# Cluster-masked attention and a maxout layer on one core: the fourth pair of the first batch gets its cluster mask another way, and VectorE shares copies in a new order

## The chip, the core and the metric

The kernel runs on one core of a Trainium2 chip. The metric is the device time of one execution, in microseconds (us). Three runs of the kernel before took 711.57, 712.71 and 713.95; the median is 712.71. Besides, one execution was recorded by the hardware profiler.

The engines are called as in the profile: PE is the matrix engine (TensorE) and PEld its loading of weights, DVE is VectorE, ACT is ScalarE, POOL is GpSimd, SP is SyncE, which only issues DMA transfers here. Each engine works through its own list of instructions in order and waits on semaphores where it needs what another one makes.

## The reference

Four batches, eight heads, 768 tokens of 64 elements. Every query and every key is assigned to the nearest of 16 centroids of its head, and a query sees only the keys of its own cluster:

```
q_assign = argmax(einsum('bhsd,hcd->bhsc', q / |q|, c / |c|), -1)
k_assign = argmax(einsum('bhsd,hcd->bhsc', k / |k|, c / |c|), -1)
scores = where(q_assign[..., :, None] == k_assign[..., None, :], q @ k.T / 8, -1e9)
x = softmax(scores) @ v            # as rows of tokens: 3072 x 512
h = maximum(maximum(x @ w1, x @ w2), x @ w3)      # 3072 x 768
out = h @ w_out                                   # 3072 x 512
```

All is float32. The kernel multiplies in float16 and splits numbers into an upper half (the float16 cast) and a lower half (what the cast left over), with a power of two as scale for each tensor, so that products of halves add up to about float32.

## The kernel before

**Tiling.** A *pair* is two heads of one batch; a batch has four. The 768 queries are six tiles of 128; a batch has two blocks of three tiles. A *visit* is one pair and one block: 32 visits, first the four pairs of block one of a batch, then those of block two, with six *steps* each (two heads by three tiles), 192 in all.

**A step** (`tile_units`, L1145). PE makes the scores of 128 queries against 768 keys in a two-bank PSUM tile `big`, of which there are three (L1160, L1162; the second adds the lower halves and the mask). DVE takes the row's maximum and writes the shifted scores back (L1171), ACT takes the exponential (L1177) and the row sum, ACT casts the upper half `hl` (L1180), and DVE or POOL subtract it for the lower half (L1183). SP then turns both halves with a transposing DMA (L1186), and the attention product (L1111) reads them. For the even steps below 40 (`BY_PE`), PE turns the float32 rows instead (L1208), and ACT (L1214) and DVE (L1216) take the halves out of PSUM into `pt`. In later batches the rows are also divided by their sum (POOL or ACT L1227, or within L1233 and L1236).

**A pair's preparation** (`prep`, L624, and `mask_rows`, L485). q and k are loaded as two tiles `stage` with the elements of q and k in the partitions and the tokens along the row. DVE or ACT takes the maximum of the absolute values, a short chain of one-column instructions (`pow2_units`, L374 to L400, with one tiny matmul) makes a power of two out of it, the halves are written to `qk` (L710 to L727). For the mask, the pair's centroids are multiplied with the `stage` tiles: in batch 0 by four float32 matmuls with the centroids `cwf` as weights (L700), which give the scores with clusters in the partitions in a `big` tile. On DVE follow: a 32 by 32 block transpose (L497), so that the 16 scores of a token lie along a row, the maximum (L506), the subtraction of it (L509), the rank of the first that equals it (L515, L518), the one-hot row (L522), its scaling to 0 or a large negative number in two copies (L535) and a block transpose back (L546). Four row copies put the result under the q and k rows of `qk`, where the score product adds it: by DVE for the very first pair (`fast`, L567), by DMA for all others (L569). `cl_t` and `cl_m` are the tiles of this chain.

**Weights and the feed-forward part.** `weights` (L956) brings the three hidden matrices in 18 pieces: loads, an upper-half cast (`top`, L928 or L930), a conversion to float32 on DVE (`wf`, L934), scaling, halves (L891, L893, L950). After the four visits of a block follows `ffn` (L1249) for its 384 tokens: 18 hidden products on PE into a one-bank PSUM tile `one`, of which there are two (L1291), each evacuated by ACT (the first of three, L1303) or DVE (with the maximum over the three, L1305), the halves of the result, three output products (L1343), their evacuation (L1353) and the store (L1357). Eight such blocks.

**What sets the order.** The code does not issue instructions as it runs. `add` records a *unit* with its dependencies and tiles; when all are recorded, `Plan.run` issues them in the sequence of the table `ORDER`, a list of unit numbers written out in the file. A unit that more than one engine may do gives its costs as a dictionary, such as `{"POOL": 1.6, "DVE": 0.85}`; then a letter of the table `HANDS` names its engine (V is DVE, S is ACT, G is POOL, Q is SP). Costs and due times in the calls of `add` have no effect on the issued order, which is all in the two tables. A tile is taken from its pool when the first unit that uses it is issued and comes free after the last, so the order also decides which of three `big` tiles a step waits for.

Of the kernel before, what the change touches and what calls it, by code (L numbers as in the profile page):

```python
# [27 lines left out]
1 0 18 19 52 51 2-5 7 6 8-13 153 417 155 14 15 20-23 30 24 16 17 54 53 39 25 55 26 29 56 40 27 57 63 58 28 41  # L28
33 31 59 42 34 43 32 73 60 44 61 45 62 74 154 36 37 67 64 68 65 38 35 85 86 176 75 69 76 156 46 157-159 50 49
# [13 lines left out]
1148 224 221 316 230 317 1158 318 1118 234 232 1119 1149 1167 319 1171 1168 320-322 233 1150 1155 1172 323 326  # L43
329 1169 1173 330 327 324 1120 325 331 1156 1177 1178 1170 1179 235 1189 1183 1180 1159 1190 1184 236 1174
1185 1181 1186 1160 1175 328 1187 237 254 257 1161 1182 238-240 1162 1191 255 256 260 1195 241 1209 419 418
242 1196 243 1210 1163 1164 258 244 259 1188 280 1197 1198 1201 251 261 252 1221 2637 1192 2639 1211 1193 248
245 253 246 249 2638 1222 420 1202 421 1199 262 263 1194 247 250 1215 422 1212 1223 281 1213 1216 423 2640 264
282 265 427 424 1214 425 266 283 1176 1224 1203 267 1227 1217 1218 1204 1225 284 285 426 268-270 1228 286 1200
# [196 lines left out]
def kernel(  # L245
# [42 lines left out]
    W_0, W_STEP = 8, 1.2  # L288
    AV_PRIO = -1.5
    F_0, F_SPAN = 7, 19  # L290
    BY_PE = set(range(0, 40, 2))
    POOL_1 = 24
    BLOCKS = [((0, 3), (3, 3)), ((0, 3), (3, 3)), ((0, 3), (3, 3)), ((0, 3), (3, 3))]

# [74 lines left out]
    def by_pool(step):  # L369
        return step % 2 if step >= POOL_1 else 1  # L370

# [1038 lines left out]
```

## Time and profile before

| | |
|---|---|
| runs, us | 711.57, 712.71, 713.95 |
| profiled execution, us | 713.19 |
| its span, first to last instruction | 711.4 |
| first score product (L1160) starts | 23.05 |
| first attention product (L1111) starts | 54.2 |
| first hidden product (L1291) starts | 109.9 |
| first hidden product of the second block starts | 204.05 |
| PE's last instruction ends | 707.6 |

The profiler's page counts an engine as busy while an instruction runs on it; matmuls are pipelined, so a busy PE is not always one at its peak. A row such as `L1183 DVE TENSOR_TENSOR hl<-e,hl 128x768 f16<-128x768 f32 x5 | 4.8, 966 | 0.0` reads: line 1183 on DVE, output tile and input tiles, 128 partitions by 768 elements with their types, five instructions, 4.8 us busy, 966 ns on average, and 0.0 us of idle time ahead of them. Behind that idle time stands what ended it. A row of a timeline begins with the start and the duration in us. Rows of several stretches give for each the length, then the busy time of each engine with its number of instructions, then the clock that PE was granted (1.00 is full speed), the share of time in which the DMA engines were busy, and GB/s.

In the forty slices of the page a digit is the busy share of some 18 us in tenths. DVE is busy 570.9 us of the span, ACT 531.4, POOL 380.6. The last chain of work runs over the output product and its evacuation (L1343, L1353) to the last store.

### The profile page before, as it was taken

How to read it: one execution, taken by the hardware profiler on the slowest of the kernel's cores; microseconds unless marked ns; L12 is line 12 of the kernel's file. 1: busy time of each engine (PE TensorE's matmuls, PEld its weight loads, DVE VectorE, ACT ScalarE, POOL GpSimd, SP SyncE). 2: the span in 40 equal slices, each digit the busy share in tenths (PEclk: the TensorE clock that was granted, in tenths of full speed). 3: DMA queues.
4: the chain of work that ended last, by engine and by line, in shares of the span. 5: the costliest groups of instructions: out<-in, count | busy, mean ns of one | idle time of the engine just before them, and what ended most of it. 6: DMA issues, size and time to landing. Idle time of an engine off the chain costs nothing. (4 is left out here: it accounts for less than half of the span.)

```text
span 711.4 us, 13113 instructions
## 1 busy us (share of the span) xinstructions
PE 666.8 (94%) x4461; PEld 384.1 (54%) x4461; DVE 570.9 (80%) x1439; ACT 531.4 (75%) x920; POOL 380.6 (53%) x363
## 2 busy tenths in 40 slices
PE   4578788998999999999999999999999999999997
PEld 1245455655566655565465555665556545564663
DVE  7989989999998866999899777999899977782120
ACT  6989889998977678789787677887787876673111
POOL 2566876768667443868456634875366421432010
PEclk9678879999999999999999999999999999999999
DMA  6779958798999979999999898999998896887001
GB/s 238 227 152 208 216 144 202 191 205 165 184 186 180 189 156 199 199 170 218 192 192 185 170 194 174 186 198 204 197 201 164 142 161 115 149 158 131 1 1 59
DMA packets 297795, 121.03 MB, mean 170 GB/s; under 512 B 273024, under 2 KB 284160, under 8 KB 297728
## 3 DMA queue, kind: packets, MB, share of 16 engines
q1 hardware_dynamic: 297728, 120.20, 82.4%
q8 instruction: 35, 0.57, 0.3%
q14 instruction: 32, 0.26, 0.1%
HBM read 31.49 MB, written 6.29 MB: 53 GB/s over the span
## 5 line engine op out<-in xcount | busy, mean ns | idle before, releaser
L1171 DVE TENSOR_SCALAR_CACHE_REDUCE big<-big,nsc 128x768 f32<-128x768 f32 x192 | 192.8, 1017 | 20.3 <-PE big L1162 18.6
L1291 PE MATMUL one<-x,w16a 128*128 128x384 f16 x1152 | 197.4, 326 | 0.2 <-ACT xs L1126 0.2
L1183 POOL TENSOR_TENSOR hl<-e,hl 128x768 f16<-128x768 f32 x80 | 133.4, 1670 | 70.3 <-ACT hl L1180 62.6
L1291 PEld LDWEIGHTS <-w16a 128*128 128x128 f16 x1152 | 111.8, 98 | 76.0 <-issue 1.9
L1177 ACT ACTIVATE e<-big,nm 128x768 f32<-128x768 f32 x116 | 104.4, 900 | 37.0 <-DVE big L1171 23.6
L1160 PE MATMUL big<-qk 128*128 128x512 f16 (+1 forms) x384 | 98.6, 340 | 14.5 <-ACT e L1177 7.2
L1111 PE MATMUL big<-pt,v 128*64 128x384 f16 x1152 | 100.2, 327 | 1.4 <-DVE hl L1183 0.5
L1291 PE MATMUL one<-x,w16b 128*128 128x384 f16 x576 | 98.9, 326 | 0.1
L1162 PE MATMUL big<-qk 96*128 96x512 f16 (+1 forms) x384 | 98.5, 338 | 0.3 <-DVE qk L567 0.3
L1180 ACT CAST hl<-e 128x768 f16<-128x768 f32 x96 | 79.7, 830 | 11.0 <-POOL e L1227 10.3
L1111 PEld LDWEIGHTS <-v 128*64 128x64 f16 x1152 | 67.5, 110 | 32.0 <-issue 8.5
L1227 POOL TENSOR_SCALAR e<-e,rs 128x768 f32<-128x768 f32 x44 | 40.4, 919 | 80.3 <-DVE rs L1198 70.9
L1177 ACT ACTIVATE big<-big,nm 128x768 f32<-128x768 f32 x76 | 66.3, 873 | 21.7 <-DVE big L1171 16.3
L1236 DVE SCALAR_TENSOR_TENSOR hl<-big,rs,hl 128x768 f16<-128x768 f32 x72 | 72.9, 1013 | 11.4 <-ACT hl L1233 10.6
L1291 PEld LDWEIGHTS <-w16b 128*128 128x128 f16 x576 | 55.9, 98 | 37.9 <-issue 1.1
L1233 ACT ACTIVATE hl<-big,rs 128x768 f16<-128x768 f32 x72 | 64.5, 898 | 15.1 <-ACT big L1177 6.1
L1160 PEld LDWEIGHTS <-qk 128*128 128x128 f16 x384 | 34.4, 99 | 48.1 <-issue 21.2
L1162 PEld LDWEIGHTS <-qk 96*128 96x128 f16 x384 | 39.0, 101 | 28.5 <-issue 3.6
L727 POOL TENSOR_TENSOR qk<-stage,qk 128x768 f16<-128x768 f32 x27 | 44.4, 1653 | 12.5 <-ACT qk L724 11.9
L1343 PE MATMUL one<-wo,vf_h 128*128 128x512 f16 x216 | 48.1, 379 | 0.6 <-ACT o L1353 0.6
L1343 PE MATMUL one<-wo,wf_h 128*128 128x512 f16 x216 | 48.3, 379 | 0.0
L1305 DVE SCALAR_TENSOR_TENSOR wf_h<-one,wf_h 128x384 f32<-128x384 f32 x48 | 26.5, 553 | 25.8 <-PE one L1291 24.4
(177 smaller groups left out, 962.7 us busy)
## 6 DMA issues: line engine op xcount, KB each, us to landing
stage<-in_qk_dram SPq DMA_DIRECT2D x32, 384.0 KB, 4.2
wd<-in_moe_w_dram SPq DMA_DIRECT2D x18, 512.0 KB, 4.4
out_dram<-o SPq DMA_DIRECT2D x24, 256.0 KB, 3.0
qk<-qk SPq DMA_DIRECT2D x30, 192.0 KB, 3.5
qk<-qk SPq DMA_DIRECT2D x15, 384.0 KB, 4.8
stage<-in_v_dram SPq DMA_DIRECT2D x12, 384.0 KB, 3.9
wd<-in_moe_w_out_dram SPq DMA_DIRECT2D x6, 512.0 KB, 4.0
qk<-cl_t SPq DMA_DIRECT2D x60, 48.0 KB, 2.5
```

Source lines behind the costliest of these rows:

```text
L727: eng.tensor_tensor(t()[:, AQ, i], x(), t()[:, BQ, i], op=ALU.subtract)
L1111: nc.tensor.matmul(t()[D * i : D * i + D, 0:nb], v()[:, i, kt, a], pts[i % len(pts)]()[:, rows[i], c * QT + kt, :], start=(m == 0), stop=( ...
L1160: nc.tensor.matmul(t()[:, lo:hi], aq[:, qs], ak[:, lo:hi], start=True, stop=False)
L1162: nc.tensor.matmul(t()[:, lo:hi], bq[0:K2, qs], bk[0:K2, lo:hi], start=False, stop=True)
L1171: nc.vector.tensor_scalar(s, s, -SCALE if exact else nscs[:, b, pr : pr + 1], 3.0e38, op0=ALU.mult, op1=ALU.min, accum_out=nm())
L1177: nc.scalar.activation(e(), t()[:, 0:S], AF.Exp, bias=nm(), scale=-1.0, accum_out=r)
L1180: nc.scalar.copy(hl()[:, 0, :], e())
L1183: eng.tensor_tensor(hl()[:, 1, :], e(), hl()[:, 0, :], op=ALU.subtract)
L1233: nc.scalar.activation(hl()[:, 0, :], e(), AF.Copy, scale=r())
L1236: eng.scalar_tensor_tensor(hl()[:, 1, :], e(), r(), hl()[:, 0, :], op0=ALU.mult, op1=ALU.subtract)
L1291: nc.tensor.matmul(t()[:, 0:nb], w16[jt // JA][:, jt % JA, wa, i, ct], x16[b, gi, ct]()[:, xa, 0:nb], start=(m == 0), stop=(m == 3 * CT - 1),)
L1343: nc.tensor.matmul(t()[:, 0:DM], h16(jt)[:, ha, tt * P : (tt + 1) * P], wo16[0][:, jt, wa, :], start=(m == 0), stop=(m == 3 * JT - 1),)
```

## The change

The lines of the kernel after differ from those before: L1171 becomes L1267, L1183 becomes L1279, L1208, L1214 and L1216 become L1304, L1310 and L1312, L893 becomes L989, L934 becomes L1030, L950 and L1046 become L1046 and L1142, L1291 becomes L1413, L930 becomes L1026, L1160 becomes L1256. A helper `scaled` now issues casts and copies, on its lines 378 and 380 for ACT and 382 for DVE and POOL.

*First*, pair 3 of batch 0 (`NEW`) takes its mask through a new function, `first_rows`. Its cluster scores come from twelve float32 matmuls with a `stage` tile's 128 tokens as weights and 32 columns of centroids (`cwn`) as the moving side, so that tokens lie in the partitions at once; they go to a one-bank tile `one` and not to a `big` one. The centroids of the old kind, `cwf`, are left for three pairs. The two block transposes go: DVE takes the maximum, compares, POOL or DVE multiplies by the ranks, DVE takes the maximum and writes both copies of the one-hot row at once in float16; PE turns these rows by six float16 transposes with a new identity `identh`, and ACT or DVE takes them out of PSUM while it scales them.

```
+    BY_16 = set()
+    NEW = {3}
...
+        cl = one() if new else big()
...
+        def cluster_raw():
+            for n in range(QT):
+                for i in range(2):
+                    at = 2 * C * (2 * n + i)
+                    w = cwn[:, 2 * (pr - len(old)) + i].rearrange("p a c -> p (a c)")
+                    nc.tensor.matmul(
+                        cl()[:, at : at + 2 * C], xs[i]()[:, n * P : (n + 1) * P], w, start=True, stop=True
+                    )
...
+    def first_rows(base, fast, cl, u, ct, cols, bc):
+        tt = one()
...
+        def same():
+            x = cl()[:, 0 : n24 * C].rearrange("p (n c) -> p n c", c=C)
+            nc.vector.tensor_tensor(eq(), x, bc(cols("cl_m")), op=ALU.is_equal)
...
+        def hot():
+            rb = rank.rearrange("p (o r c) -> p o r c", o=1, r=1).broadcast_to([P, n24, 2, C])
+            m = cols("cl_m2").rearrange("p (n r o) -> p n r o", r=1, o=1).broadcast_to([P, n24, 2, C])
+            nc.vector.tensor_tensor(oh().rearrange("p (n r c) -> p n r c", r=2, c=C), rb, m, op=ALU.is_equal)
+
+        def turn():
+            for n in range(QT):
+                r = slice(n * P, (n + 1) * P)
+                nc.tensor.transpose(tt().bitcast(F16)[:, r], oh()[:, r], identh)
...
+        u = add("DVE", 0.47, red, [u], [cl, ct], base)
+        u = add("DVE", 0.47, same, [u], [cl, ct], base)
+        u = add({"POOL": 0.87, "DVE": 0.47}, 0, ranks, [u], [ct], base, port=True)
+        u = add("DVE", 0.46, red2, [u], [ct], base)
+        u = add("DVE", 0.87, hot, [u], [ct], base, port=True)
+        u = add("PE", 0.42, turn, [u], [ct, tt], base)
+        return add({"ACT": 0.78, "DVE": 0.53}, 0, take, [u], [ct, tt], base)
```

*Second*, many units that ACT (or ACT and POOL) did may now also run on DVE or POOL, by `HANDS`: casts of upper halves, scalings, copies out of PSUM, the first evacuation of three in the feed-forward part, the output's evacuation.

```
+    def scaled(eng, out, x, k=1.0):
+        if eng is nc.scalar:
+            if isinstance(k, float) and k == 1.0:
+                eng.copy(out, x)
+            else:
+                eng.activation(out, x, AF.Copy, scale=k)
+        else:
+            eng.tensor_scalar(out, x, k, 1.0, op0=ALU.mult, op1=ALU.mult)
...
-        u = add("ACT", 0.74 if pool else 0.8 if norm else 0.71, hi, [u], held, step)
+        ways = {"ACT": 0.73, "POOL": 0.91, "DVE": 0.47} if pool else {"ACT": 0.79 if norm else 0.69, "DVE": 0.94 if norm else 0.86}
+        u = add(ways, 0, hi, [u], held, step, port=pool)
...
-            h = add("ACT", 0.71, lambda: nc.scalar.copy(part(0), o()[:, 0:S]), [u], [o, pt], step)
+            h = add({"ACT": 0.69, "DVE": 0.86}, 0, lambda eng: scaled(eng, part(0), o()[:, 0:S]), [u], [o, pt], step)
...
-                u = add("DVE" if i else "ACT", 0.07 + 0.4 * share if i else 0.1 + 0.3 * share, ev, deps, [t, tmp], prio - 2)
+                ways = {"DVE": 0.07 + 0.4 * share}
+                if not i:
+                    ways["ACT"] = 0.08 + 0.3 * share
+                u = add(ways, 0, ev, deps, [t, tmp], prio - 2)
```

In the same way the casts of q, k, v, `xs`, `x` and weight halves, the scalings, the row copies of the first pair and the moves of its rows (`m0` to `m3`) get further engines. By the new table the moves stay on ACT, and of the four row copies three go to ACT and one stays on DVE.

Over the whole kernel, casts of upper attention halves into `hl` from SBUF go from 96 on ACT to 71 on ACT, 21 on POOL and 4 on DVE; those out of PSUM from 72 on ACT to 63 on ACT and 9 on DVE; the first evacuations of three from 48 on ACT to 36 on ACT and 12 on DVE.

*Third*, `pow2_units` drops two one-column instructions where the maximum is a single column already: the reduction, and the last scaling by 2^14, which is now folded into the floor. The constant of the output's scale is changed to match, and `ident16` is a view of `ident`.

```
+        def floor(x=cols):
+            nc.vector.tensor_scalar(m(), x() if callable(x) else x, 1e-30, 2.0**-14, op0=ALU.max, op1=ALU.mult)
+
+        if not multi:
+            part = [(0.06, floor), (0.06, cut)]
...
-            (0.06, lambda: nc.vector.tensor_scalar_mul(s(), s(), 2.0**14)),
```

*Fourth*, `ORDER` and `HANDS` are new throughout. `BY_16` is empty, so the code for steps turned in float16 by PE issues nothing. No DMA is added or removed.

On DVE, where the fourth pair of batch 0 gets its mask (the tiles `cl_t` with a number, `cl_m` and `onehot` are that pair's), stood before:

```order
L1171 TENSOR_SCALAR big,nm<-big,nsc 128x768
L518 TENSOR_REDUCE cl_m_697<-cl_t_443 128x24
L1216 TENSOR_TENSOR pt<-big,pt 128x768
L1096 RECIPROCAL rs<-rs 128x6
L1171 TENSOR_SCALAR big,nm<-big,nsc 128x768 x2
L522 TENSOR_TENSOR cl_t_443<-rank,cl_m_697 128x24x16
L934 SCALAR_TENSOR_TENSOR wf<-wd,top 128x512
L535 TENSOR_SCALAR onehot_99<-cl_t_443,ksel 128x768
L546 STREAM_TRANSPOSE cl_t_443<-onehot_99 128x768
L1171 TENSOR_SCALAR big,nm<-big,nsc 128x768
```

and now, where the pair's chain starts from PSUM (`cl_m<-one`):

```order
L527 TENSOR_REDUCE cl_m<-one 128x24
L1267 TENSOR_SCALAR big,nm<-big,nsc 128x768
L1312 TENSOR_TENSOR pt<-big,pt 128x768
L1267 TENSOR_SCALAR big,nm<-big,nsc 128x768
L531 TENSOR_TENSOR cl_t_474<-one,cl_m 128x384
L1267 TENSOR_SCALAR big,nm<-big,nsc 128x768
L1192 RECIPROCAL rs<-rs 128x6
L1267 TENSOR_SCALAR big,nm<-big,nsc 128x768
L382 TENSOR_SCALAR pt<-big 128x768
L1312 TENSOR_TENSOR pt<-big,pt 128x768
L1030 SCALAR_TENSOR_TENSOR wf<-wd,top 128x512
L538 TENSOR_REDUCE cl_m_475<-cl_t_474 128x24
```

The scaling and the transpose are gone from the chain, its links lie further apart between the score steps, and DVE has a cast out of PSUM (L382, into `pt`) that ACT did before.

On POOL, from some 70 us of the profile of before on, up to the attention output of the second pair (`x_853`; `w16a` is a weight half, `v` a half of v), stood:

```order
L1183 TENSOR_TENSOR hl<-e,hl 128x768 x2
L950 TENSOR_TENSOR w16a<-wf,w16a 128x512 x2
L808 TENSOR_TENSOR v_666<-vf,v_666 128x12x64
L1183 TENSOR_TENSOR hl<-e,hl 128x768
L950 TENSOR_TENSOR w16a<-wf,w16a 128x512
L930 CAST top<-wd 128x512
L1183 TENSOR_TENSOR hl<-e,hl 128x768
L947 TENSOR_SCALAR wf<-wf,sc_s 128x512
L1046 TENSOR_TENSOR x_853<-xs,x_853 128x384
```

and at the like place (the second pair's output is `x_877`):

```order
L989 TENSOR_SCALAR w16a<-wf 128x512
L1046 TENSOR_TENSOR w16a<-wf,w16a 128x512
L382 TENSOR_SCALAR hl<-e 128x768
L1279 TENSOR_TENSOR hl<-e,hl 128x768 x2
L1046 TENSOR_TENSOR w16a<-wf,w16a 128x512
L989 TENSOR_SCALAR x_877<-xs 128x384
L382 TENSOR_SCALAR hl<-e 128x768
L1279 TENSOR_TENSOR hl<-e,hl 128x768
L1142 TENSOR_TENSOR x_877<-xs,x_877 128x384
```

At this place POOL now also makes upper halves of attention rows (L382, `hl<-e`), each followed by a lower half (L1279), and upper halves of weights and of `x` (L989).

More of the change, by code (lines that the diff above doesn't have):

```diff
@@ L413 @@
     c2 = first.tile([P, 2, D], F32, name="c2")
-    cwf = first.tile([P, H, D], F32, name="cwf")
-    nc.gpsimd.memset(cwf, 0.0)
+    old = [pr for pr in range(NPAIR) if pr not in NEW]
+    if old:
+        cwf = first.tile([P, 2 * len(old), D], F32, name="cwf")
+        nc.gpsimd.memset(cwf, 0.0)
+    if NEW:
+        cwn = first.tile([P, 2 * len(NEW), 2, C], F32, name="cwn")
+        nc.gpsimd.memset(cwn, 0.0)
+    kbig = const([P, 1], F32, "kbig")
+    nc.gpsimd.tensor_scalar(kbig, ksel, -BIG, 1.0, op0=ALU.mult, op1=ALU.mult)
     if RAW:
@@ L468, in cwf_take @@
         tv = c_t()[:, 0:P].rearrange("p (r i c) -> p r i c", i=2, c=C)
-        cv = cwf.rearrange("p (r i) x -> p r i x", i=2)
+        n = len(old)
+        assert old == list(range(n)), "the later pairs are the new ones"
         for a in range(2):
             rows = slice(D * a, D * a + D)
-            nc.vector.tensor_copy(cv[rows, :, :, 32 * a : 32 * a + C], tv[rows])
+            if old:
+                cv = cwf.rearrange("p (r i) x -> p r i x", i=2)
+                nc.vector.tensor_copy(cv[rows, :, :, 32 * a : 32 * a + C], tv[rows, 0:n])
+            if NEW:
+                cv = cwn.rearrange("p (r i) a c -> p r i a c", i=2)
+                nc.vector.tensor_copy(cv[rows, :, :, a], tv[rows, n:])
         if RAW:
@@ L693, in prep, with cluster_old @@
         raw = b == 0
-        cl = big()
-        def cluster_raw():
+        new = raw and pr in NEW
+        cl = one() if new else big()
+        def cluster_old():
             for c0, c1 in HALF:
@@ L808, in lo @@
             eng.tensor_tensor(v()[:, :, :, 1, :], xv, v()[:, :, :, 0, :], op=ALU.subtract)
-        u = add("ACT", 0.74, hi, [u], extra + [v], in_prio)
+        u = add({"ACT": 0.72, "POOL": 0.91, "DVE": 0.47}, 0, hi, [u], extra + [v], in_prio, port=True)
         u_v[b, pr] = add({"POOL": 1.6, "DVE": 0.85}, 0, lo, [u], extra + [v], in_prio, port=True)
@@ L841, in sc @@
                     eng.tensor_scalar(y, y, s(), 1.0, op0=ALU.mult, op1=ALU.mult)
-            k = add({"ACT": 0.84, "POOL": 0.95}, 0, sc, [u], [x[pr // 2], s], prio)
+            k = add({"ACT": 0.84, "POOL": 0.95, "DVE": 0.46}, 0, sc, [u], [x[pr // 2], s], prio, port=True)
             part = lambda pr=pr: x[pr // 2]()[:, (pr & 1) * S : (pr & 1) * S + S]
@@ L867, in sc @@
                 eng.tensor_scalar(x(), x(), s(), 1.0, op0=ALU.mult, op1=ALU.mult)
-        u = add({"POOL": 0.87, "ACT": 0.84}, 0, sc, [u], [x, s], prio - 3)
+        u = add({"POOL": 0.87, "ACT": 0.84, "DVE": 0.53}, 0, sc, [u], [x, s], prio - 3, port=True)
         v_tail(b, pr, x, u, prio - 2, [x])
@@ L950, in low @@
             eng.tensor_tensor(lo(), x(), hi(), op=ALU.subtract)
-        u = add({"POOL": 0.67, "ACT": 0.62}, 0, sc, deps, [x_lease, s_lease], prio)
-        u = add({"ACT": 0.53, "POOL": 0.6}, 0, half(hi, x), [u], [x_lease], prio)
+        u = add({"POOL": 0.67, "ACT": 0.62, "DVE": 0.39}, 0, sc, deps, [x_lease, s_lease], prio, port=True)
+        u = add({"ACT": 0.53, "POOL": 0.6, "DVE": 0.33}, 0, half(hi, x), [u], [x_lease], prio, port=True)
         return add({"POOL": 1.12, "DVE": 0.6}, 0, low, [u], [x_lease], prio, port=True)
@@ L1050, in av_cost @@
     def av_cost(gn):
-        return {1: 1.7, 2: 2.1, 3: 2.9}[gn]
+        return {1: 1.7, 2: 2.1, 3: 3.06}[gn]
     def visit(n, b, pr, gi):
@@ L1138, in visit @@
         u_h = add(
-            {"POOL": 0.05 + 0.43 * k, "ACT": 0.1 + 0.3 * k}, 0, half(lambda: x()[:, 0, 0:nb], xr), [u], [xs, x], p,
+            {"POOL": 0.05 + 0.43 * k, "ACT": 0.1 + 0.3 * k, "DVE": 0.06 + 0.2 * k}, 0, half(lambda: x()[:, 0, 0:nb], xr), [u], [xs, x], p, port=True,
         )
@@ L1227, in sc, with hi @@
                     eng.tensor_scalar(e(), e(), r(), 1.0, op0=ALU.mult, op1=ALU.mult)
-            u = add({"POOL": 0.87, "ACT": 0.84}, 0, sc, [u], [ex, rs], step)
+            u = add({"POOL": 0.87, "ACT": 0.84, "DVE": 0.53}, 0, sc, [u], [ex, rs], step, port=True)
         elif norm:
-            def hi():
-                nc.scalar.activation(hl()[:, 0, :], e(), AF.Copy, scale=r())
+            def hi(eng):
+                scaled(eng, hl()[:, 0, :], e(), r())
             def lo(eng):
```

254 lines of the change are left out of this document (159 added, 95 removed), and 209 rows, old and new, of the table ORDER.

## The prediction

> **What bounds the kernel now.** I read the busy shares and the slices of the page first, then three stretches, then who keeps TensorE waiting, then the instruction groups of the stretch in which it waits.
>
> ```profile
> span 711.4 us, 13113 instructions
> PE 666.8 (94%) x4461; PEld 384.1 (54%) x4461; DVE 570.9 (80%) x1439; ACT 531.4 (75%) x920; POOL 380.6 (53%) x363
> PE   4578788998999999999999999999999999999997
> PEclk9678879999999999999999999999999999999999
> 204.05 2.11 PE L1291 MATMUL one<-x,w16a 128*128 128x384 f16 x12
> 0.00:110.00 110.00, 77.62 (x447) 42.76 (x448) 98.07 (x212) 93.02 (x161) 68.75 (x88) 0.81 0.76 195
> 110.00:204.00 94.00, 86.98 (x627) 52.18 (x626) 91.38 (x237) 87.46 (x158) 70.44 (x68) 1.00 0.87 194
> 204.00:707.60 503.60, 502.21 (x3390) 289.16 (x3388) 381.44 (x992) 350.24 (x602) 241.36 (x209) 1.00 0.84 161
> PE big L1160 <- ACT e L1177: 7.2, 7, 1.7
> PE big L1160 <- DVE pt L1216: 5.3, 5, 1.9
> ```
>
> The stretch rows hold the busy time of PE, PEld, DVE, ACT and POOL, then the granted clock, the DMA share and GB/s. From 204 us on TensorE is idle 503.60 - 502.21 = 1.4 us: nothing there can be gained, only lost. All of its waiting lies ahead of 204.05 us, where the second feed-forward block starts: 32.4 us up to 110 and 7.0 us up to 204. In these two stretches DVE is busy 98.07 of 110 and 91.38 of 94, ACT 93.02 and 87.46, POOL 68.75 and 70.44. The waits of the last two rows are for the exponentials and for the low halves that empty a score bank, so for ACT and DVE. **The elementwise engines, DVE first, set when the second block can start; what follows is 507.4 us of TensorE work and the tail.** The order of TensorE's own work is nearly unchanged: 56 score tiles, 8 attention products and 18 hidden products stand ahead of that point before and after.
>
> **The change part by part.** I counted each engine's instructions up to that point in the two orders and priced them with the group rows of 0 to 204 us.
>
> ```profile
> L1183 DVE TENSOR_TENSOR hl<-e,hl 128x768 f16<-128x768 f32 x5 | 4.8, 966 | 0.0
> L808 DVE TENSOR_TENSOR v<-vf,v 128x768 f16<-128x768 f32 x2 | 2.6, 1280 | 0.0
> L497 DVE STREAM_TRANSPOSE cl_t<-big 128x768 f32<-128x768 f32 x7 | 6.8, 976 | 1.1 <-PE big L700 1.1
> L546 DVE STREAM_TRANSPOSE cl_t<-onehot 128x768 f16<-128x768 f16 x6 | 5.8, 970 | 0.0
> L515 DVE SCALAR_TENSOR_TENSOR cl_t<-cl_t,rank 128x384 f32<-128x384 f32 x6 | 3.3, 553 | 0.0
> L522 DVE TENSOR_TENSOR cl_t<-rank,cl_m 128x384 f16<-128x384 f32 x6 | 3.5, 581 | 0.0
> L535 DVE TENSOR_SCALAR onehot<-cl_t,ksel 128x768 f16<-128x768 f16 x6 | 2.4, 406 | 0.0
> L567 DVE COPY qk<-cl_t 32x768 f16<-32x768 f16 x4 | 1.4, 352 | 0.1
> L384 DVE TENSOR_REDUCE sc_m<-wmx 128x1 f32<-128x1 f32 x6 | 0.9, 144 | 0.0
> L396 DVE TENSOR_SCALAR sc_s<-sc_s 128x1 f32<-128x1 f32 x10 | 1.5, 151 | 0.2
> L1216 DVE TENSOR_TENSOR pt<-big,pt 128x768 f16<-128x768 f32 x20 | 18.9, 949 | 0.0
> L1305 DVE SCALAR_TENSOR_TENSOR vf_h<-one,vf_h 128x384 f32<-128x384 f32 x12 | 6.6, 550 | 0.1
> L713 DVE SCALAR_TENSOR_TENSOR qk<-stage,q_s,qk 128x768 f16<-128x768 f32 x2 | 2.0, 1014 | 0.0
> L934 DVE SCALAR_TENSOR_TENSOR wf<-wd,top 128x512 int32<-128x512 int32 x24 | 18.0, 752 | 0.5 <-POOL top L930 0.5
> L950 DVE TENSOR_TENSOR w16a<-wf,w16a 128x512 f16<-128x512 f32 x2 | 1.5, 772 | 0.0
> ```
>
> *DVE loses*: five low halves of attention rows, 5 x 0.966 = 4.83; two low halves of v, 2 x 1.280 = 2.56; three mask copies, 3 x 0.352 = 1.06; eight reductions and ten scalings of one column, 8 x 0.144 + 10 x 0.151 = 2.66. The fourth pair's mask loses both transposes (0.976 + 0.970), the pick (0.553), the one-hot (0.581) and its scaling (0.406), 3.49 in all, and gains a comparison (0.57, as the one-hot) and a one-hot of twice the width, between 0.58 and 1.16, taken as 1.0: 1.92 saved. Together 13.0 us.
>
> *DVE gains*: six casts of 768 columns out of PSUM. The nearest row is L1216, also from PSUM: 6 x 0.949 = 5.7. One evacuation of 384 columns, 0.55; one low half of weights, 0.77. Casts from SBUF to SBUF of float32 by one input stand in no row. For the one of 768 columns the bounds are 0.406 (L535) and 1.014 (L713), and I take 0.6. For the four of 512 they are 0.406 x 512/768 = 0.27 and 0.752 (L934), and I take 0.4, nearer to L535, which also has one input. Together 5.7 + 0.55 + 0.77 + 0.6 + 1.6 = 9.2, between 8.5 and 11.1.
>
> Net DVE: 13.0 - 9.2 = **3.8 us less** (1.9 to 4.6). The ends of neighbouring instructions overlap a little, so I take 3.5.
>
> *ACT and POOL* share the rest:
>
> ```profile
> L1180 ACT CAST hl<-e 128x768 f16<-128x768 f32 x26 | 21.6, 832 | 0.9 <-POOL e L1227 0.7
> L928 ACT CAST top<-wd 128x512 f16<-128x512 bf16 x12 | 9.3, 775 | 0.2 <-DVE rs L1096 0.2
> L719 ACT ACTIVATE stage<-stage,q_s 128x768 f32<-128x768 f32 x7 | 6.5, 935 | 0.1
> L1183 POOL TENSOR_TENSOR hl<-e,hl 128x768 f16<-128x768 f32 x21 | 35.6, 1698 | 12.2 <-ACT hl L1180 8.5 <-issue 3.4
> L721 POOL TENSOR_SCALAR stage<-stage,q_s 128x768 f32<-128x768 f32 x5 | 4.5, 904 | 4.4 <-ACT pt L1214 3.5 <-DVE q_s L681 0.9
> ```
>
> ACT gives up 16 casts of 768 columns (seven of attention rows, four of turned rows, three of v, two of q/k), 16 x 0.832 = 13.3, and small weight casts. It takes on five upper-half casts, 5 x 0.775 = 3.9, four scalings, 4 x 0.935 = 3.7, and three mask copies of 0.35 to 1.47 (a long copy of 1536 columns takes 1.47 there, below): about 4 us less. POOL takes on five casts of attention rows, 5 x 0.904 = 4.5, four low halves, 4 x 1.698 = 6.8, two of v, 3.4, and five casts of v and q/k, 4.5. It gives up five upper halves and nine scalings and small casts: 8 to 11 us more on its 139.2. It stays the least busy of the three, so I cost this at nothing; if that cover is gone, a tile whose cast and low half both run on POOL reaches its transposing DMA 0.9 us later, and the attention product behind it as well.
>
> *TensorE*: the fourth pair's cluster scores become twelve small products, and six float16 turns are new.
>
> ```profile
> L1208 PE MATMUL big<-ident,e x120: 270/273/477, 29.4 to 150.0; 128*128 128x128 f32 x120
> 37.39 2.83 PE L700 MATMUL big<-stage,cwf 128*64 128x512 f32 x8
> 62.12 1.54 PE L1208 MATMUL big<-ident,e 128*128 128x128 f32 x6
> 66.78 1.48 PE L1208 MATMUL big<-ident,e 128*128 128x128 f32 x6
> 21.53 1.47 ACT L753 COPY qk<-qk 64x1536 f16<-64x1536 f16 x1
> ```
>
> The old scores took 2.83. Twelve products that each load 128 float32 rows cost at least half of two L1208 groups (1.5) and at most twice the old group (5.7); I take two groups, 3.1. The turns cost up to 1.5. That is some 1.5 us more, and TensorE waits 32.4 us in this stretch: hidden. If the score tile behind the twelve products is the one DVE waits for, up to 3 us shows. In exchange they use a small bank, and a score bank is no longer held by this pair. No DMA is added; the fourth pair's copies are issued as before, behind a mask that is ready earlier.
>
> *Behind 204 us* DVE takes on about 23 us (evacuations, casts and scalings that ACT and POOL gave up), 381 + 23 of 504. TensorE is still the fuller engine, so I cost it at nothing. If an evacuation comes late, TensorE stands still, since only two banks hold its products.
>
> **Sum.** The profiled execution took 713.19 us: the span of 711.4 and 1.79 around it. Less 3.5 it is 709.7. The median shown, 712.71, lies 0.48 below that execution, so the forecast is **709.2 us**.
>
> **The rivals.** *No difference (712.5).* The waits are handoffs: score to exponential to low half to bank. With three banks these chains have the same links as before, and the time saved becomes idle time of DVE, which has 11.9 us idle up to 110 already. For it: the rows of 7.2 and 5.3 us, single waits of up to 1.9. Against it: DVE is 97% busy from 110 to 204.
>
> *More (704).* ACT loses some 4 us as well, and the freed score bank shortens the waits of 7.2 and 5.3 us. If four tenths of these 12.5 us go too, 709.2 less 5.0 is 704.
>
> *Slower (717).* DVE and POOL hinder each other:
>
> ```profile
> 41.76 1.65 POOL L1183 TENSOR_TENSOR hl<-e,hl 128x768 f16<-128x768 f32 x1
> 42.59 1.62 DVE L808 TENSOR_TENSOR v<-vf,v 128x768 f16<-128x768 f32 x1
> L808 DVE TENSOR_TENSOR v<-vf,v x2: 939/1280/1622, 30.4 to 42.6; 128x768 f16<-128x768 f32 x2
> ```
>
> The DVE instruction that starts at 42.59 under a running POOL instruction takes 1.62, the same one alone 0.94: 0.68 lost. DVE has 57 instructions with two SBUF inputs or a plain SBUF copy up to 204 us (63 before), and POOL runs 8 to 11 us more. Five more such meetings eat the 3.5 us; at twelve (8.2 us) the kernel is 4.7 us slower, 717.4. Against it: most groups that could meet POOL have means near their lone times (0.966 for L1183), and there are six fewer of them.
>
> The Trainium skill bears on this rival: its page "SBUF — State Buffer", section "Who interferes with whom", says that a DVE instruction in a two-port mode or with two SBUF inputs and a GpSimd instruction that reads SBUF hold a shared port pair by turns, each for its whole length, and the later one blocks. By that rule every new SBUF copy on DVE is a candidate on either side. The rows of 41.76 and 42.59 agree: 42.59 + 1.62 ends 0.8 us after POOL's 43.41, about a lone instruction.
>
> **How the numbers follow.** Forecast 0.40 (its own range 706 to 710.5); more 0.18; no difference 0.24; slower 0.18. A measurement of this kernel tells some 0.3%, 2.1 us, from no change: faster 0.58, same 0.24, slower 0.18. The range reaches from the better part of the third case to the worst of the last, 703 to 717, and leaves out about a tenth at either end.
>
> **What would show it.** Right: the second block's first hidden product starts near 200.5 us, the time from it to the end stays near 507.4, and DVE's low halves of attention rows and the tiny columns are gone from the early stretch. Wrong on DVE: that start comes earlier or later by several us, or DVE idles more ahead of it. The lock shows as DVE copies well above 0.6 us. Loss behind 204 us shows as more than 2 us of TensorE idle time there. The mask step is right if the fourth pair's products take about 3.1 us.

## The result, and the profile after

The kernel after takes 719.16 us (five runs, 718.56 to 722.69), the one before 712.71 (711.57 to 713.95): the ratio is 1.0105, 95% interval 1.0085 to 1.0125. It is 6.5 us slower, outside the range of 703 to 717 that was given. The profiled execution took 718.62 us, its span is 716.8.

The page of the kernel after, its span, busy times and TensorE's slices:

```profile
span 716.8 us, 13118 instructions
PE 668.5 (93%) x4483; PEld 384.9 (54%) x4483; DVE 601.9 (84%) x1450; ACT 495.2 (69%) x864; POOL 400.7 (56%) x375
PE   3766888999999999999999999999999999999997
```

DVE is busy 31.0 us longer than before (570.9), ACT 36.2 us less, POOL 20.1 us longer. The three stretches of the prediction, with the same columns, and the first hidden product of the second block in TensorE's timeline:

```profile
0.00:110.00 110.00, 78.00 (x480) 44.88 (x480) 101.62 (x209) 91.89 (x163) 77.82 (x95) 0.89 0.80 201
110.00:204.00 94.00, 86.97 (x614) 50.50 (x614) 91.81 (x224) 83.84 (x150) 73.58 (x66) 0.98 0.80 185
204.00:713.00 509.00, 503.49 (x3391) 289.51 (x3389) 408.46 (x1018) 318.74 (x553) 249.26 (x215) 1.00 0.84 160
204.22 2.11 PE L1413 MATMUL one<-x,w16a 128*128 128x384 f16 x12
```

Two things are to be seen. *The start has not moved*: 204.22 us against 204.05, though DVE was to have 3.5 us less to do ahead of it. Its busy time there rose, from 98.07 + 91.38 = 189.5 to 193.4 us. *In this pair of profiles the whole loss lies behind it*: from the start to the end of the span 512.6 us pass instead of 507.4, and TensorE idles 509.00 - 503.49 = 5.5 us there, before it was 1.4. These 4.1 us are most of the 5.2; the other 1.1 stand in TensorE's busy time (503.49 instead of 502.21), and no view here says why. Each profile is one execution. The time behind the start hardly differs between profiles: it is 506.7 to 507.4 us in five with the old order there, 512.6 here and 513.4 in the kernel with five exchanges below. The start differs more, as the experiments show.

Where DVE's 13 us went shows in its groups ahead of 204 us (count, busy us and mean ns, idle time before):

```profile
L1030 DVE SCALAR_TENSOR_TENSOR wf<-wd,top 128x512 int32<-128x512 int32 x24 | 21.5, 895 | 0.8 <-POOL top L1026 0.6 <-ACT top L1024 0.3
L595 DVE SCALAR_TENSOR_TENSOR cl_t<-cl_t,rank 128x384 f32<-128x384 f32 x5 | 4.6, 918 | 0.0
L382 DVE TENSOR_SCALAR pt<-big 128x768 f16<-128x768 f32 x4 | 3.8, 941 | 0.1
L757 DVE SCALAR_TENSOR_TENSOR nsc<-q_p 128x1 f32<-128x1 f32 x7 | 2.3, 329 | 0.0
L543 DVE TENSOR_TENSOR cl_t<-rank,cl_m 128x768 f16<-128x768 f32 x1 | 0.9, 949 | 0.0
L382 DVE TENSOR_SCALAR qk<-stage,q_s 128x768 f16<-128x768 f32 x1 | 0.6, 598 | 0.0
```

The added instructions cost about what was estimated: the cast out of PSUM 0.941 (0.949 was taken), the double one-hot 0.949 (1.0), the cast from SBUF 0.598 (0.6). One added instruction is not in the sum, the low half of an attention output (L1142, `x<-xs`), which POOL made before; DVE has it at 201.76 us for 1.27. And the weight conversion, unchanged and of unchanged number, has a mean of 895 ns instead of 752, and the rank product 918 instead of 553. The timelines of DVE and POOL show single ones:

```profile
51.88 1.65 POOL L818 TENSOR_TENSOR qk<-stage,qk 128x768 f16<-128x768 f32 x1 [0.66 <-ACT qk L378]
51.96 2.11 DVE L1030 SCALAR_TENSOR_TENSOR wf<-wd,top 128x512 int32<-128x512 int32 x1
70.01 1.64 POOL L1279 TENSOR_TENSOR hl<-e,hl 128x768 f16<-128x768 f32 x1
70.05 2.15 DVE L1030 SCALAR_TENSOR_TENSOR wf<-wd,top 128x512 int32<-128x512 int32 x1
41.19 1.64 POOL L904 TENSOR_TENSOR v<-vf,v 128x768 f16<-128x768 f32 x1
41.43 1.41 DVE L757 SCALAR_TENSOR_TENSOR nsc<-q_p 128x1 f32<-128x1 f32 x1
```

Each DVE row starts just behind the start of a POOL low half and ends when that one has ended or half a microsecond later: 70.01 + 1.64 = 71.65, and 70.05 + 2.15 = 72.20. In the kernel with five exchanges, below, the one-column scale of the last row has a mean of 0.148. I added up, over all single rows of DVE ahead of 204 us, what exceeds the form's usual time (its lower quartile) by more than 0.15 us: 2.9 us in 6 rows before, 9.4 us in 10 rows after. Below this sum is called the *lengthening*. The Trainium skill says in "SBUF — State Buffer", section "Who interferes with whom", that a DVE instruction with two SBUF inputs and a GpSimd instruction that reads SBUF hold a shared port pair by turns, each for its whole length; these rows agree, also for a scale of a single column. Every lengthened row of both profiles lies under an instruction of POOL.

Behind 204 us TensorE waits at nine places; the six largest (engine, line, what it waited for; us, times, longest):

```profile
PE one L1413 <- ACT o L380: 1.3, 1, 1.3
PE big L1256 <- issue: 1.0, 1, 1.0
PE big L1256 <- DVE rs L1293: 0.7, 1, 0.7
PE big L1256 <- PE big L1207: 0.6, 1, 0.6
PE one L1413 <- DVE vf_h L1427: 0.6, 1, 0.6
PE big L835 <- DVE hl L1332: 0.5, 1, 0.5
```

The largest in the timeline of ACT and PE:

```profile
664.84 0.58 ACT L380 ACTIVATE x<-big,cv 128x384 f16<-128x384 f32 x1 [10.13 <-PE big L1207]
665.32 1.26 ACT L380 ACTIVATE o<-one,so 128x512 f32<-128x512 f32 x2
666.05 1.62 PE L1413 MATMUL one<-x,w16a 128*128 128x384 f16 x9 [1.25 <-ACT o L380]
```

ACT stood idle for 10.13 us with two finished output products waiting, since the copy of the last attention product stood ahead of them in its list. They hold both `one` banks, so the last feed-forward block starts 1.25 us late.

### The profile page after: what moved, and what is told of

The parts are those of the page before. It is cut to its first block, busy times and chain, and to the rows that moved or that the text cites. A ratio compares the mean times of both kernels' runs of the same rounds, so it can differ in the third digit from the quotient of the medians.

```text
span 716.8 us, 13118 instructions
## 1 busy us (share of the span) xinstructions
PE 668.5 (93%) x4483; PEld 384.9 (54%) x4483; DVE 601.9 (84%) x1450; ACT 495.2 (69%) x864; POOL 400.7 (56%) x375
## 5 line engine op out<-in xcount | busy, mean ns | idle before, releaser
L1267 DVE TENSOR_SCALAR_CACHE_REDUCE big<-big,nsc 128x768 f32<-128x768 f32 x192 | 192.9, 1017 | 13.1 <-PE big L1258 12.5
L1413 PE MATMUL one<-x,w16a 128*128 128x384 f16 x1152 | 199.1, 328 | 1.3 <-ACT o L380 1.3
L1279 POOL TENSOR_TENSOR hl<-e,hl 128x768 f16<-128x768 f32 x84 | 139.8, 1667 | 47.2 <-ACT hl L378 40.4
L1413 PEld LDWEIGHTS <-w16a 128*128 128x128 f16 x1152 | 112.3, 98 | 77.8 <-issue 4.8
L1256 PE MATMUL big<-qk 128*128 128x512 f16 (+1 forms) x384 | 98.1, 338 | 18.2 <-DVE pt L1312 7.4
L1413 PE MATMUL one<-x,w16b 128*128 128x384 f16 x576 | 98.9, 326 | 1.0 <-DVE vf_h L1427 0.6
L1413 PEld LDWEIGHTS <-w16b 128*128 128x128 f16 x576 | 55.9, 98 | 38.8 <-issue 2.2
L378 ACT CAST hl<-e 128x768 f16<-128x768 f32 x71 | 58.8, 829 | 22.4 <-POOL e L1323 12.3
L380 ACT ACTIVATE hl<-big,rs 128x768 f16<-128x768 f32 x63 | 56.6, 898 | 20.3 <-issue 9.5
L1256 PEld LDWEIGHTS <-qk 128*128 128x128 f16 x384 | 34.6, 99 | 53.7 <-issue 25.7
L1323 POOL TENSOR_SCALAR e<-e,rs 128x768 f32<-128x768 f32 x33 | 30.9, 936 | 46.1 <-DVE rs L1294 40.4
L818 POOL TENSOR_TENSOR qk<-stage,qk 128x768 f16<-128x768 f32 x28 | 47.4, 1702 | 7.9 <-ACT qk L378 5.7
L1142 POOL TENSOR_TENSOR wf_h<-wf_h 128x384 f16<-128x384 f32 x16 | 14.7, 919 | 58.8 <-ACT wf_h L987 47.4
```

The costliest lines, as they stand in the source:

```text
L378: eng.copy(out, x)
L380: eng.activation(out, x, AF.Copy, scale=k)
L818: eng.tensor_tensor(t()[:, AQ, i], x(), t()[:, BQ, i], op=ALU.subtract)
L1256: nc.tensor.matmul(t()[:, lo:hi], aq[:, qs], ak[:, lo:hi], start=True, stop=False)
L1267: nc.vector.tensor_scalar(s, s, -SCALE if exact else nscs[:, b, pr : pr + 1], 3.0e38, op0=ALU.mult, op1=ALU.min, accum_out=nm())
L1279: eng.tensor_tensor(hl()[:, 1, :], e(), hl()[:, 0, :], op=ALU.subtract)
```

## The experiments

All kernels are timed against the kernel before on the same chip; a ratio below 1 is faster than before. Most edits change only the tables `ORDER` and `HANDS`; a diff then shows instructions of an engine as they move.

**Order and engines apart.** One kernel has the new order with the old engines, one the reverse, one neither (so only the mask, the chains and the constants), one the old engines behind 204 us alone.

```diff
 ORDER new, HANDS old      (k1_order; k4_late: only for units behind the second block's first hidden product)
 ORDER old, HANDS new      (k2_engines)
 ORDER old, HANDS old      (k3_mask: NEW = {3} and the shorter chains stay)
```

> The kernel after with its new order of units, its new mask and its shorter scale chains, but each unit that has a choice of engine goes to the engine that did it before (220 letters of the table). Theory E (the new choice of engines costs the time: DVE has some 20 us more work behind 204 us, and POOL's added casts meet DVE more often): 709 to 713 us, the second block's first hidden product near 200 to 204 us, TensorE idle under 2 us behind it, DVE's lengthened instructions ahead of 204 us back from 9.4 to about 3 us. Rival O (the new order itself holds handoffs too close together): 717 us or more, with 4 to 5 us of TensorE idle behind 204 us as in the kernel after.

> The kernel after with its mask, its scale chains and its choice of engines, but issued in the order of before (each unit where its counterpart stood). Theory E: 717 to 723 us, DVE's lengthened instructions ahead of 204 us at 8 us or more. Rival O: 711 to 714 us. If both order and engines fit only each other, this and the kernel with the new order and the old engines are both above 719.

> Only the fourth pair's new mask, the shorter scale chains and the constants, in the order and with the engines of before. If DVE's work ahead of 204 us sets the start of the second block: 6.1 us less DVE work (3.5 of the mask, 2.7 of the chains, and the one-hot scaling), so 707 to 710 us. If the handoffs between score, exponential and bank set it: 712 to 713 us, TensorE's idle time ahead of 204 us unchanged at about 39 us. If the twelve small products or the fourth pair's mask come late: above 714.

> The kernel after, with the engines of before only for units that stand behind the second block's first hidden product in the order. Theory E, by DVE's load behind 204 us: 713 to 714.5 us, TensorE idle under 2 us there, the start still near 204. Rival O: 718 to 719.5 us, with the same stalls as the kernel after.

Measured: 781.23 us (ratio 1.0956, 1.0926 to 1.0986), 765.1 (1.0734, 1.0713 to 1.0756), 717.27 (1.0067, 1.0047 to 1.0087) and 749.1 (1.0529, 1.0489 to 1.0569). Neither theory E nor rival O has anything near three of the four. The expectation of the reverse kernel named a third case, which came: order and engines fit only each other. The 128 letters changed behind 204 us cost 30 us by themselves. So these three tell nothing of what the change costs. The remaining one, with the old order and the old engines, does: the mask and the chains alone make the kernel slower.

**The chains without the mask, and the mask out of the new order.** For the second, the old mask's cluster products and its first transpose were put where the new products stand.

```diff
-    NEW = {3}
+    NEW = set()
```

> Only the shorter scale chains and their constants, with the old mask, the order and the engines of before: 8 reductions and 10 scalings of one column are gone from DVE ahead of 204 us, 2.7 us by the prediction. If DVE's busy time sets the second block's start: 710 to 711 us. If the handoffs set it: 712 to 713 us. Together with the kernel that has the new mask too (717.3) it prices the mask in the old order: 4 to 7 us.

> The kernel after, its order and its engines, but with the fourth pair's old mask (four cluster products into a score bank, two block transposes on DVE). By the prediction the new mask saves DVE 3.5 us (its scaling counted) and is hidden on TensorE: then this kernel is 2 to 4 us slower than the one after, 721 to 723 us. If the new mask costs time in this order as it does in the old one: 714 to 717 us.

Measured: 711.95 us (0.9987, 0.9968 to 1.0006) with the chains alone, 1.0 below the 712.96 of the kernel before beside it, which cannot be told from none; 722.67 (1.0148, 1.0124 to 1.0171) with the old mask in the new order. By the medians the new mask costs 717.27 - 711.95 = 5.3 us in the old order and saves 722.67 - 719.16 = 3.5 us in the new one. So the same instructions cost or save by their place.

**What the mask waits for in the old order.** Its profile shows two stalls (timeline of PE and DVE of the kernel with the mask in the old order; its lines are 8 lower):

```profile
37.09 5.16 PE L783 MATMUL one<-cwn,stage 128*128 128x32 f32 x24
43.57 1.03 DVE L1259 TENSOR_SCALAR_CACHE_REDUCE big<-big,nsc 128x768 f32<-128x768 f32 x1 [4.26 <-PE big L1250]
68.75 0.95 DVE L535 TENSOR_TENSOR cl_t<-rank,cl_m 128x768 f16<-128x768 f32 x1
69.76 0.82 PE L540 MATMUL one<-identh,cl_t 128*128 128x128 f16 x6 [1.99 <-DVE cl_t L535]
```

DVE stands idle for 4.26 us for a score that TensorE makes after the twelve products, and TensorE stands 1.99 us at the first turn, until DVE has the one-hot rows. One kernel splits the products into six and six around a score tile, one moves the turns and the copy behind them past a score tile, the turned rows and the sums.

```diff
-            u_cl = add("PE", ..., cluster_raw if new else cluster_old, ld + [u_cf], xs + [cl], base)
+            u_cl = add("PE", ..., (lambda: cluster_raw(0, 3)) if new else cluster_old, ld + [u_cf], xs + [cl], base)
+            if new:
+                u_cl = add("PE", ..., lambda: cluster_raw(3, QT), [u_cl], xs + [cl], base)
```

> The kernel with only the new mask and the shorter chains in the old order (717.3), with the twelve cluster products issued as six, the next score tile, and six more. Theory B (the twelve products stand as one block of 5.2 us ahead of a score that DVE then waits 4.3 us for): the wait falls to about 2 us and the time to 714 to 715.5 us. Rival M (the mask's own chain is late for the fourth pair, or TensorE simply has more work): 717 us as before the split.

```diff
 PE, near 70 us (k13_turn)
-L548 turns x6
 L1304 MATMUL big<-ident,e x6
 L1256, L1258 one score tile
 L1199 MATMUL one<-ident,rs
+L548 turns x6
```

> The kernel with only the new mask and the shorter chains in the old order (717.3), with the six turns and the copy behind them moved past one score tile, one turn of rows and the row sums. Theory W (TensorE, which takes its list in order, stands at the first turn until DVE has the one-hot rows): the wait of 1.99 us at 69.76 is gone and the time is 714 to 715.5 us. Rival M (the twelve products ahead of it cost the whole difference): 717 to 718 us.

Measured: split 719.14 (1.0087, 1.0058 to 1.0116), not better than unsplit; turns moved 714.33 (1.0027, 1.0008 to 1.0046), 2.9 us better. TensorE's rows there now read

```profile
69.32 0.88 PE L1199 MATMUL one<-ident,rs 128*64 128x128 f32 x12
70.13 0.51 PE L548 MATMUL one<-identh,cl_t 128*128 128x128 f16 x6
```

with no wait. So, by the medians, more than half of the mask's price in the old order is a wait that it brings to TensorE's own list: what was a chain within DVE now crosses to TensorE, which takes its list in order. In the kernel after, the turns stand at 62.33 us, late enough that nothing waits. Of the other 2.4 us the products are the likely part, but it is not shown: DVE's wait of 4.26 us behind them is still there with the turns moved, and the split, which cut it to 1.70 and 1.89, did not help.

**DVE's load behind 204 us.**

```diff
 HANDS, behind the second block's first hidden product: 40 units V -> S
```

> The kernel after, with the 40 units behind the second block's first hidden product that went from ACT to DVE given back to ACT (12 upper-half casts of attention rows, 11 evacuations, 5 output casts, 5 halves, 3 output evacuations and 4 more); nothing else is changed. Theory L (DVE's extra load behind 204 us makes evacuations late): TensorE's 5.4 us of idle time there falls under 2 us and the kernel takes 713 to 715 us. Rival H (the handoffs of the new order stand too close, whoever does them, and ACT is now the one that comes late): 719 us or more, with other stalls of the same or a larger sum.

Measured: 726.1 us (1.019, 1.0153 to 1.0226). The rival held: with 40 instructions given back to ACT other stalls come, up to 1.3 us each, and the one at the last block stays. TensorE idles 10.8 us from 204 to 705 us, where it idles 5.5 in the kernel after. DVE's added work is not by itself what makes the late part slow.

**The meetings of DVE and POOL ahead of 204 us.** Five DVE instructions are exchanged with neighbours:

```diff
 DVE
-L757 nsc                             (41.43)
 L626, L527
+L757 nsc
+L1030 wf                             (51.96)
 L1312 pt<-big,pt
-L1030 wf
-L1030 wf                             (70.05, 111.15)
 L1267 big,nm
+L1030 wf
-L595 cl_t<-cl_t,rank                 (144.23)
 L1312 pt<-big,pt
+L595 cl_t<-cl_t,rank
```

> The kernel after, with five of DVE's instructions that stood 1.3 to 1.5 us under a POOL low half ahead of 204 us (the row scale at 41.43, the weight conversions at 51.96, 70.05 and 111.15, the rank product at 144.23) exchanged with a neighbour on DVE that reads PSUM. Theory P (these meetings ate the gain ahead of 204 us): DVE's lengthened instructions ahead of 204 us fall from 9.4 us to 4 to 6, and the second block starts 3 to 5 us earlier, near 200; the kernel takes 714 to 716 us if the loss behind that point stays. Rival H (handoffs set the start): the lengthening falls, but the start stays within 1 us of 204 and the time within 718 to 720.

Measured: 715.28 us (1.0033, 1.0018 to 1.0048), 3.9 us better than the kernel after. The profiled execution took 717.10 us, the longest of its eleven. Even there the lengthening ahead of 204 us is 6.0 us instead of 9.4, the group means are back, and the second block starts at 201.90, 2.3 us earlier:

```profile
L1030 DVE SCALAR_TENSOR_TENSOR wf<-wd,top 128x512 int32<-128x512 int32 x24 | 18.5, 769 | 0.4 <-issue 0.4
L757 DVE SCALAR_TENSOR_TENSOR nsc<-q_p 128x1 f32<-128x1 f32 x7 | 1.0, 148 | 0.0
201.90 2.11 PE L1413 MATMUL one<-x,w16a 128*128 128x384 f16 x12
```

**Three stalls behind 204 us.** On the same engines, three places get another order; one kernel has this alone, one together with the five exchanges, and one also mends the second place, which the first two missed (the reciprocal and the low half still stood behind the mask's chain).

```diff
 ACT, last block:  the two evacuations o<-one ahead of x<-big,cv
 ACT, near 512 us: one o<-one behind the next exponential; DVE: L1294 rs ahead of L615 onehot
 DVE, near 484 us: L1427 vf_h<-one ahead of L1267
 k12_chain besides, near 512 us: DVE L602, L615, L626 behind L1332, ACT o<-one behind hl<-big,rs
```

> The kernel after with three places behind 204 us put in another order, on the same engines: ahead of the last feed-forward block ACT evacuates two output products before it takes the last attention product (stall of 1.25 us at 666.05); near 512 us one output evacuation stands behind the next exponential and one reciprocal ahead of the mask's one-hot (0.97 us at 516.51); near 484 us DVE evacuates a hidden product before the next score (0.56 us at 485.24). Theory H (the loss behind 204 us is a handful of handoffs in which an off-path instruction stands ahead of the one that TensorE waits for, each passed on in full): the three stalls are gone, TensorE's idle time there falls from 5.4 to 2.6 to 3 us, and the time is 716 to 717 us. Rival L (DVE and ACT are too full there; each stall that goes comes back a little later): the time stays within 718 to 720.

> The three places behind 204 us and the five exchanges ahead of it together. If the two losses are separate and add up: 712 to 713 us (715.3 of the exchanges alone, less 2.5 to 2.8), the same as before. If they overlap: 714 to 716.

> The kernel with both sets of exchanges (714.8), and near 512 us the mask's one-hot, scaling and block transpose moved on DVE behind the low half that frees a score bank, the output evacuation on ACT behind the upper half. Theory H (order of instructions on one engine): the stall of 0.95 us at 516.35 falls under 0.2 and the time to 713.5 to 714.3 us. Rival L (no room): another stall of about the same size comes within 20 us, and the time stays at 714.8.

Measured: 718.07 us (1.0062, 1.0039 to 1.0085), 714.82 (1.002, 1.0002 to 1.0038) and 714.62 (1.0029, 1.0011 to 1.0048). The stall of 1.25 us at the last block is gone in all three; the one at 485 us came back as 0.4 us a little later, and the first two show a new one of 0.8 and 1.0 us near 212. The third kernel has no stall at 516 us, but its waits list holds a new one, at 518.00:

```profile
PE one L1413 <- DVE q_p L753: 1.1, 1, 1.1
```

So both theories hold in part: the stall at the end was an order of two instructions on one engine, those that DVE causes return a few us later. The three places were to bring 2.5 to 2.8 us and brought 719.16 - 718.07 = 1.1 without the exchanges and 715.28 - 714.82 = 0.5 with them, neither clear of the spread. Which part of the new order behind 204 us costs the rest stays open.

**The new first stage with the old rest.** Up to shortly before the second block (977 of 3078 units) the kernel after, behind it the order and the engines of before. The place where one order passes into the other is called the seam. Four kernels: with the five exchanges, with them and an earlier seam, without them, and with them and the seam's own stall mended.

```diff
 ORDER: the first 977 units as after (k15_hybrid1: the first 478), then all others in the sequence of before
 HANDS: new for those, old for the others
```

> The kernel after with the five exchanges up to shortly before the second block's first hidden product (977 of 3078 units), and from there on the order and the engines of before. If the two losses are the whole reason: the second block starts 2 to 4 us earlier than before, near 201, TensorE idles 1 to 2 us behind it, and the time is 709.5 to 711.5 us. If handoffs behind that point depend on how the first stage leaves the banks, or the early gain is an artefact of one profile: 712.5 to 715 us.

> The same with the seam near the first hidden product (478 units): the mask, the exchanges up to 110 us, and the order and engines of before from there on. If the gain lies ahead of the first hidden product (which starts 3 to 5 us earlier than before in the kernels with the exchanges): 708.5 to 711 us. If it lies between 110 and 204 us, or is lost there with the old order: 712 to 714 us.

> The kernel after up to the same seam (977 units), without the five exchanges, then the order and engines of before. If the meetings with POOL ate the gain of the first stage and the losses add up: 710.8 plus the 3.9 us that the exchanges brought in the new order, 713.5 to 715, no faster than before. If the late part was the whole loss: 710 to 711.5.

> The kernel with the exchanges and the old rest (710.75), with an output evacuation on ACT ahead of an upper half, and two maxima that wait for a load moved on DVE behind the row scale and the low half. The seam's stall of 1.27 us at 203.42 goes: 709.3 to 710.3 us. If DVE's load of that place brings it back elsewhere: 710.5 to 711.5.

Measured: 710.75 us (0.9962, 0.9945 to 0.9978), 711.37 (0.996, 0.9945 to 0.9976), 715.35 (1.0031, 1.0015 to 1.0047) and 711.7 (0.9975, 0.9957 to 0.9993). With the exchanges the kernel is faster than the kernel after, and by 0.4% than the one before. The earlier seam fell between its two theories. For the first of the four, the stretch from 204 us to the end of TensorE's work, and the second block's first hidden product:

```profile
204.00:704.80 500.80, 499.63 (x3374) 286.59 (x3372) 379.80 (x968) 348.30 (x600) 241.40 (x208) 1.00 0.83 161
200.04 2.11 PE L1413 MATMUL one<-x,w16a 128*128 128x384 f16 x12
```

The start is 4.0 us earlier than before, and TensorE idles 500.80 - 499.63 = 1.2 us behind 204 us. Just ahead of that stretch, at 203.42, the seam costs a wait of 1.3 us; mending it brought nothing that can be told.

Four kernels now stand in a square:

| us | new order behind 204 us | old order behind 204 us |
|---|---|---|
| without the exchanges | 719.16 | 715.35 |
| with the five exchanges | 715.28 | 710.75 |

The exchanges bring 3.9 and 4.6 us, the old rest 3.8 and 4.5: the two losses add up, and either alone leaves the kernel slower than before. Three cautions belong to this. The kernel without exchanges and with the old rest waits 2.3 us at the seam, 1.0 more than the one with them, so up to 1 us of the 4.6 may belong to the seam. And the exchanges change when things stand in line, not only the meetings; that the meetings are what counts is read from the rows and not shown by a run of its own.

The third caution is that the lengthening is not fixed by the order. Five profiled kernels have the first stage of the kernel after (the last of them but for its last few instructions):

| kernel | lengthening ahead of 204 us | the twelve cluster products, us | second block starts |
|---|---|---|---|
| after | 9.4 | 3.19 | 204.22 |
| three places behind 204 us in another order | 8.8 | 5.16 | 205.31 |
| 40 units given back to ACT | 7.1 | 2.76 | 200.36 |
| old engines behind 204 us | 5.9 | 2.76 | 199.78 |
| old rest, without the exchanges | 5.5 | 5.16 | 201.37 |

```profile
205.31 2.11 PE L1413 MATMUL one<-x,w16a 128*128 128x384 f16 x12
199.78 2.11 PE L1405 MATMUL one<-x,w16a 128*128 128x384 f16 x12
```

The starts differ by 5.5 us and go with the lengthening, though not strictly; the products show that TensorE's rate, of which the last section tells, differs between them too. In five profiles with the exchanges (and the seam at 977 units or none) the lengthening is 4.8 to 6.0 us and the start 200.04 to 203.04. In the old order with the old mask it is 2.9 in the kernel before and 6.1 with the chains alone. So the pair of 2.9 and 9.4 shows the growth near its largest, and how much of the 3.9 us that the exchanges bring comes from the meetings stays open.

## Why the prediction was wrong

- *What bounds the kernel*: right in part. Where the start of the second block moved, in the kernels with the exchanges, the time followed. But DVE's busy time alone does not set that start: with the mask in the old order DVE is busy 184.06 us up to 204, 5.4 less than before, and the block starts later, at 208.48, since DVE waits for TensorE.
- *DVE's instructions, net 3.8 us less*: the counting held but for one instruction of 1.27 us, and the prices held. Busy time less the lengthening went from 189.5 - 2.9 = 186.6 to 193.4 - 9.4 = 184.0 us, 2.6 us less, within the bounds of 1.9 to 4.6. **The step that failed is the sum's silence on meetings**: it priced each instruction by its mean of before, as if the new order would meet POOL as seldom as the old. In the two profiled executions the lengthening grew by 6.5 us and more than ate the gain; other profiles of the new first stage show 5.5 to 8.8 us of it instead of 9.4. The rival "Slower" had this mechanism, with its point of decision (five meetings) and its price (0.68 each, 8.2 us for twelve), but its argument against itself was wrong: with six fewer such DVE instructions, POOL 12 us busier and less idle time on both engines, ten rows were lengthened instead of six. Single meetings cost up to 1.5 us, not 0.68; in the rows shown these are the ones in which the DVE instruction started within 0.1 us of POOL's, or was a tiny one that waited nearly all of POOL's.
- *The fourth pair's mask*: 1.92 us were expected of it on DVE, and 3.5 us is what the old mask costs in the new order. The twelve products took 3.19 us in the profiled execution (3.1 were taken), the turns 0.51. That the size came out is luck: in ten other profiles of the new first stage, with the exchanges or without, the same products took 5.16 or 5.17 us in seven, near the upper bound of 5.7, and 2.76 in three. The wait for a score tile behind them was named (up to 3 us; 4.26 in the old order). The wait that the turns add to TensorE's list was not named at all; the new order hides it, the old one does not.
- *The chains*: 2.66 us of DVE time, 1.0 us of the kernel's, with an interval that holds no gain as well as 2.3 us. The runs do not tell whether the chains are worth their busy time.
- *ACT and POOL at nothing*: POOL rose by 12.2 us where 8 to 11 was said. Its room was there; by the rows shown, what it cost was DVE's time.
- *Behind 204 us at nothing*: **the second step that failed**, and the larger one by its price, 512.6 - 507.4 = 5.2 us. The 27.0 us more of DVE work lay under TensorE's by the busy shares, but nine handoffs did not, 5.5 us of idle time instead of 1.4. The old rest brings 3.8 and 4.5 us of it back, so the loss belongs to the new order and engines there; mending the largest stalls did not, so which of its handoffs are to blame is not shown. The sentence on late evacuations named the mechanism and gave it no price and no chance. An average of 408 in 509 us says nothing of the instant at which a bank is wanted.
- *More* and *No difference*: the first needs a start near 196 us, the second holds for the first stage alone, for another reason: the time saved did not turn to idle time of DVE, in the profiled execution it turned to lengthening.

## What to carry to other kernels

Where an order is rewritten, an engine's work is not the sum of its instructions' lone times: look up which of them share a port with a neighbour, price the meetings from the worst row, not from the first that shows one, and read more than one profile before calling their sum a property of the order. Work that moves onto a second engine brings a wait into that engine's list; name what stands behind it there. A stage in which the bound engine is busy 99.7% can only lose, so every instruction added beside it needs its deadline checked, not its share of busy time.

## What the runs showed of the hardware

TensorE runs much of the first 120 us in spells at half its rate, and these differ from execution to execution. From 40 to 50 us the granted clock is 0.84 in the kernel before, 0.50 in the kernel after. In the kernel with the mask in the old order the score products of one form read (TensorE's timeline, then three stretches):

```profile
44.72 0.84 PE L1248 MATMUL big<-qk 128*128 128x512 f16 x2
48.08 0.50 PE L1248 MATMUL big<-qk 128*128 128x512 f16 x2 [0.67 <-DVE pt L1304]
66.33 0.80 PE L1248 MATMUL big<-qk 128*128 128x512 f16 x2 [1.54 <-DVE pt L1304]
20.00:50.00 30.00, 24.29 (x93) 14.60 (x89) 24.85 (x55) 25.20 (x42) 16.92 (x13) 1.00 0.67 181
60.00:70.00 10.00, 4.96 (x26) 2.42 (x26) 9.53 (x20) 9.43 (x18) 7.01 (x6) 0.82 1.10 219
66.00:68.00 2.00, 1.44 (x4) 0.40 (x3) 1.53 (x5) 1.97 (x5) 1.75 (x2) 0.58 1.00 271
```

The pair takes 0.84 us at 44.72 and 0.50 at 48.08, while the granted clock of 20 to 50 us is 1.00: the column does not show this first slow spell. It does show the one that begins at 66.33, with 0.58 from 66 to 68 us. So early in a profile the durations of one form are the better sign. The same twelve cluster products took 2.76, 3.19 or 5.16 us in different profiles of the new order. Most kernels here spread over 4 us from run to run, and these spells are a likely reason beside the meetings; no run tried it. The Trainium skill, in "TensorE: Matmul & The Clock Gate", Part 1, says that the array falls to half rate after an idle window of about 3.4 us, and that the moment at which it comes to full rate varies between runs; the half rate agrees with these rows, but in that kernel a spell begins at 66.33 us, and the longest wait in the 10 us ahead of it is 1.54, well below that figure.
